# Other column blocks, later selection rounds, a split copy and a reordered first chunk in a retention and soft-MoE kernel

## The chip, the core and the metric

The kernel runs on one core of a Trainium2 chip. The metric is the device time of one execution in microseconds. A profiled execution also gives a span, from the first to the last instruction of the program on the core; the device time is a little longer than the span. All times on a trace below count from the start of the span.

The engines are named as the profile names them: PE is TensorE (matmuls; PEld is its weight load), DVE is VectorE, ACT is ScalarE, POOL is GpSimd, and SP is SyncE, which issues every DMA here. PSUM is the memory that PE writes its results to.

## The reference

Two layers stand behind each other. The first is a retention layer for 4 batches, 8 heads, 768 tokens and head size 64, in which a state per head decays by a factor gamma at each token:

```python
for t in range(S):
    state = gamma * state + k[:, :, t] (outer) v[:, :, t]
    y[:, :, t] = q[:, :, t] @ state / sqrt(D)
```

Its output, with the heads side by side, is x with 3072 tokens of 512 columns. The second layer is a soft mixture of 8 experts with 4 slots each:

```python
logits = x @ phi                               # 3072 x 32
d = softmax(logits, over the tokens)
slot_input = d.T @ x                           # 32 x 512, 4 slots per expert
slot_out = relu(slot_input @ w1[e]) @ w2[e]    # 512 -> 1024 -> 512
c = softmax(logits, over the 32 slots)
out = c @ slot_out                             # 3072 x 512
```

All data is fp32. The weights w1 and w2 have 16.8 MB each, and the output, which the kernel writes transposed as 512 x 3072, has 6.3 MB.

## The kernel before, in words

**Retention.** The work is cut into 24 steps (`NSTEP`): 4 batches of 6 chunks, each of 128 tokens. A step loads three things: `load_kq(i)` brings k and q transposed (512 KB, into one of four tiles `kq`), `load_v(i)` brings v (256 KB, into a tile `h`) and, in some steps, k in its natural order (another 256 KB). On POOL v is then scaled by the decay (L207); for chunk 0 the scaling is split between POOL and DVE instead (L428 to L430). `scores(i)` makes the products of k and q on PE (L225), and DVE multiplies them by a mask (L229) into a tile that `intra(i)` multiplies with v on PE (L258). `inter(i)` adds the part of the carried state (L247), `scale(i)` scales the result on DVE (L267), `state(i)` updates the state (L280, L282), and `natural(i)` transposes the 128 x 512 block of x on PE (L288) and copies it out of PSUM (L290): on ACT for all steps, except for the last step, which uses DVE.

**Routing.** After each group of four steps `logits_mm` and `logits` make the slot logits, with a running maximum, and `dispatch_p` and `dispatch_u` add the group's part of the slot inputs: four matmuls (L342), each of which needs one step's copied x. The last group is finished after the loop, at about 109 to 117 us, and gives the slot inputs `siT` (L520). `combine_weights` makes the combine weights c of a group.

**Experts.** `hidden(g, k)` multiplies the slot inputs with the tiles of w1 (L533): two halves g of four experts each, with four k each. After the last k of a half its two PSUM tiles are copied out, one by ACT (L539) and one by DVE (L540). `hidden_t(g)` transposes the hidden layer (L546) and applies the relu on DVE (L551).

**Selection rounds.** The output matmuls want c with a token along the free axis and a slot pattern along the partitions. `split_c` splits c on DVE into two parts (L384, L385). `c_round(n)`, for n from 0 to 3, multiplies them on PE with selection matrices (L395) into two PSUM tiles named `sm`, of which there are two, and ACT copies them to the tiles `c4T` (L401): four copies in rounds 0 and 1 (which serve the first 2048 tokens), two in rounds 2 and 3. Two rounds in a row thus need the same two `sm` tiles, and a round's matmuls wait until ACT has copied the round before.

**Blocks of columns.** The second expert layer and the output go by blocks of output columns, `BLOCKS`: 128, then 256, then 128. The tiles of w2 are stored and loaded in the order of the blocks. For each block PE runs 64 matmuls (L623: two halves of experts, eight steps `fc` over the 1024 hidden values, four experts each) into one PSUM tile, which needs all of that block's w2. `finish(cb, op)` is a generator that then does the rest: a copy on DVE (L586), a summing matmul (L590), a cast and a subtraction on DVE (L592, L593), and then the output matmuls (L605), two for each output tile of 128 columns by 1024 tokens. Their results are copied by DVE (first half, L611) and ACT (second half, L608), and SP writes the tile of 512 KB to HBM (L609). So a block of 128 columns has 6 output matmuls and 3 writes, and a block of 256 has 12 and 6. Each `yield` of the generator lets the next block run one `fc` step of four matmuls; `Y1` and `Y2` say how many steps lie before the summing matmul and before the first output matmul, and `BURST` says that output matmuls go in threes. When a block's matmuls are through, what is left of the generator before is drained.

**What sets the order.** The order on PE is the order of the code (`ORDERED`). On the other engines a scheduler sets the order when the program is built. Each engine runs its queue in order. SP issues the loads in its queue's order; the ring for weights has 34 tiles of 512 KB (`NRING`), and four more weight loads go to the `kq` tiles and six to pairs of `h` tiles.

Of the kernel before, what the change touches and what calls it, by code (L numbers as in the profile page):

```python
# [12 lines left out]
ALU = mybir.AluOpType  # L13
# [4 lines left out]
C = 128  # L18
# [16 lines left out]
HLOAD = 4  # L35
ORDERED = {mybir.EngineType.PE}
NPRE = 34
BLOCKS = [(0, 128), (128, 256), (384, 128)]
NRING = 34
NHALF = 20  # L40
NSPLIT = 6
# [2 lines left out]
KLOAD = [i for i in range(1, NSTEP) if i % NC in (0, 2, 4)]  # L44
KQW = 1088
FPS = {256: 4, 192: 4, 128: 8, 64: 8}
Y1 = (3, 4, 2)
Y2 = (4, 6, 2)
GRP = 4
NGRP = NSTEP // GRP  # L50

# [40 lines left out]
def retention_soft_moe_kernel(  # L92
# [117 lines left out]
    def scores(i):  # L210
        s = st[i]
        state = i % NC < NC - 1 and i not in KLOAD
        A = s["A"] = [half_tile().rearrange("p (r g t) -> p r g t", r=2, t=C) for _ in range(2)]
        if state:
            s["kn"] = half_tile().rearrange("p (h e) -> p h e", e=D)
        for hf in range(2):
            scv = sct[hf][:, :, 0:384].rearrange("p r (g n) -> p r g n", n=192)
            for gg in range(2):
                g = 2 * hf + gg
                for late in range(2):  # L220
                    for r in range(2):
                        o = (late if g % 2 == 0 else 1 - late) * D
                        kb = KB[2 * g + late]
                        n = 2 + state - late
                        nc.tensor.matmul(scv[o:o + D, r, gg, late * D:(late + n) * D],  # L225
                                         s["kq"][r * D:(r + 1) * D, kb * D:(kb + 1) * D],
                                         blocks(s["kq"], r, NB - (2 - late) * QS[g], QS[g], n),
                                         start=True, stop=True)
            nc.vector.tensor_tensor(A[hf], scv[:, :, :, 0:C],  # L229
                                    mask.unsqueeze(1).broadcast_to([128, 2, 2, C]), ALU.mult)  # L230
            if state:
                kn = s["kn"].rearrange("p (g r) e -> p r g e", r=2)[:, :, 2 * hf:2 * hf + 2]
                nc.scalar.copy(kn, scv[:, :, :, C:C + D])  # L233
# [50 lines left out]
    def natural(i):  # L284
        s = st[i]
        xp = ps.tile([128, DM], F32, name="misc")
        for g in range(NPAIR):
            nc.tensor.transpose(xp[:, g * 128:(g + 1) * 128], s["yT"][:, g, :], ident)  # L288
        s["xn"] = half_tile()
        (nc.vector.tensor_copy if i == NSTEP - 1 else nc.scalar.copy)(s["xn"], xp)  # L290

    gs = {}

# [43 lines left out]
    def dispatch_u(g):  # L337
        q = gs[g]
        last = g == NGRP - 1
        u = ps.tile([128, DM], F32, name="y1" if last else "misc")  # L340
        for j in range(GRP):
            nc.tensor.matmul(u[32 * j:32 * j + 32, :], q["p"][:, 32 * j:32 * j + 32], st[GRP * g + j]["xn"],  # L342
                             start=True, stop=True, tile_position=(0, 32 * j))
        if g == 0:
            nc.scalar.copy(acc, u)
        elif last:
            q["u"] = ysc.rearrange("p g t -> p (g t)")
            for k in range(NK):
                ks = slice(k * 128, (k + 1) * 128)
                nc.scalar.copy(q["u"][:, ks], u[:, ks])  # L350
        else:
            nc.vector.scalar_tensor_tensor(zrun, zrun, q["al"], q["z"], ALU.mult, ALU.add)
            nc.vector.scalar_tensor_tensor(acc, acc, q["al"], u, ALU.mult, ALU.add)


    def combine_weights(g):
# [68 lines left out]
                         nc.const_aps.tensor(0.0, [128, WN], WDT), start=True, stop=True)  # L425
    pe_ = [None]
    scores(0)
    for e, hs_ in ((nc.gpsimd, slice(4, 8)), (nc.vector, slice(0, 4))):  # L428
        e.tensor_tensor(st[0]["v"][:, hs_], st[0]["v"][:, hs_],
                        vsc[:, 0, hs_].unsqueeze(2).broadcast_to([128, 4, D]), ALU.mult)  # L430
    budget = 0.0
    for i in range(NSTEP):
        last = i == NSTEP - 1
# [132 lines left out]
    load_weights(4)  # L566
    hidden(1, 1)
    hidden_t(0)
    c_round(0)
    for k in (2, 3):  # L570
        load_weights(4)
        hidden(1, k)
        c_round(k - 1)
    load_weights(len(weights))
    c_round(3)


    co_tags = [(pe, "sm", 2), (ps, "misc", 1), (ps, "y1", 1), (pe, "sm", 2), (ps, "S", 1)]
# [37 lines left out]

    for cb, (c0, w) in enumerate(BLOCKS):
        op = pe.tile([128, 512], F32, name=("sc0", "sc1")[cb % 2])
        for g in range(2):
            for fc in range(NFC):  # L620
                for j in range(4):
                    t, f = w2t[4 * g + j, cb][2 * fc // FPS[w]], fc % (FPS[w] // 2)
                    nc.tensor.matmul(op[32 * j:32 * j + 32, :w], hT[fc // 2][:, fc % 2, 4 * g + j, :],  # L623
                                     t[:, f * w:(f + 1) * w],
                                     start=(g == 0 and fc == 0), stop=(g == 1 and fc == NFC - 1),
                                     skip_group_check=True, tile_position=(0, 32 * j))
                if cb == 0 and g == 0 and fc == 2:
                    hidden_t(1)
                for f in pend:
                    next(f, None)  # L630
        done = finish(cb, op)
        next(done)
        for f in pend:
            for _ in f:
                pass
        pend = [done]
# [59 lines left out]
```

## Time and profile before

| | us |
|---|---|
| device time, median of 3 runs | 175.55 |
| lowest and highest of them | 175.05, 176.4 |
| device time of the profiled execution | 174.94 |
| its span | 173.0 |
| PE busy | 149.7 (86%) |
| DVE busy | 93.2 (54%) |
| ACT busy | 48.1 (28%) |
| DMA queue of the program, share of 16 engines | 92.9% |

The DMA engines moved 62.51 MB in the span, 361 GB/s on average. PE is busy in most of the span as well. A share over the whole span does not tell which of the two ends last in a stage; for that the span is cut into stages, and in each the waits and the DMA share are read. Three views are used: the busy time by windows, the instructions of one engine in order of time (with the idle time before each, and what ended it), and the chain of work that ended last. A line of the time order gives start and duration in us, engine, line, operation, what is written and read, and how many instructions are merged; a time in square brackets is the idle time before it. On PE an fp32 matmul is recorded as two instructions.

### The profile page before, as it was taken

Reading aid. Unit: us, or ns where it says so; the run is one execution under the profiler, and the core shown is the slowest. Engines: PE = TensorE matmul, PEld = TensorE weight load, DVE = VectorE, ACT = ScalarE, POOL = GpSimd, SP = SyncE. Lnnn points to the kernel's source line nnn. Section 1 sums busy time; section 2 is a strip of 40 time slices with the busy share of each in tenths; the row PEclk is TensorE's granted clock in tenths of the full one; section 3 lists DMA queues with packets and bytes.
Section 4 is the critical chain, followed back from the end, with each engine's and each line's share of the span. In section 5 each row is a group of like instructions: output and inputs, shape, how many; then the busy total and the mean of one; then the engine's idle time right before and its main releaser. Section 6 shows DMA issues by size and latency. Waiting matters only on the chain.

```text
span 173.0 us, 6469 instructions
## 1 busy us (share of the span) xinstructions
PE 149.7 (86%) x2752; PEld 106.4 (62%) x2752; DVE 93.2 (54%) x278; ACT 48.1 (28%) x122; POOL 31.9 (18%) x46
## 2 busy tenths in 40 slices
PE   8589966999899999979999799999977898999700
PEld 2378955689669767868679668853322493566500
DVE  1566645777876787757775685434132131425720
ACT  2133322343513342324133422310102700303510
POOL 0243214213331322031421322400200000000000
PEclk9999999999999999999999999999999999999985
DMA  5999999999999999999999998999999999444993
GB/s 186 322 408 390 368 403 408 403 392 403 402 397 405 403 401 407 396 405 401 403 403 402 406 405 330 279 352 328 357 412 418 410 405 367 184 194 175 393 405 123
DMA packets 20765, 62.51 MB, mean 361 GB/s; under 512 B 2304, under 2 KB 2688, under 8 KB 20736
## 3 DMA queue, kind: packets, MB, share of 16 engines
q1 hardware_dynamic: 20736, 62.09, 92.9%
q8 instruction: 22, 0.36, 0.9%
q14 instruction: 7, 0.06, 0.1%
HBM read 55.79 MB, written 6.29 MB: 359 GB/s over the span
## 4 chain that ended last, share of the span: by engine, by line
PE 69%; DMA 13%; DVE 6%; issue 5%; SPq 1%; ACT 1%; DVEq 0%
PE y L258 11%; PE sc L225 10%; PE sc L623 9%; PE misc L288 7%; PE y L247 5%; DMA kq<-in_kq_dram 5%; DMA r<-in_w_dram 5%; PE y L533 4%; PE S L280 4%; DMA h<-in_v_dram 3%; PE misc L300 3%; PE misc L342 2%; PE misc L533 2%; PE S L533 2%; PE sm L605 2%
## 5 line engine op out<-in xcount | busy, mean ns | idle before, releaser
L229 DVE TENSOR_TENSOR h<-sc,kt 128x512 f32<-128x512 f32 x48 | 31.4, 686 | 18.6 <-PE sc L225 14.6
L207 POOL TENSOR_TENSOR h<-h,kt 128x512 f32<-128x512 f32 x23 | 24.1, 1049 | 61.8 <-DMA h<-in_v_dram 46.3
L267 DVE SCALAR_TENSOR_TENSOR h<-y,kt,ysc 128x128 f32<-128x128 f32 x96 | 27.3, 343 | 4.5 <-PE y L258 4.2
L258 PE MATMUL y<-h 128*64 128x128 f32 x384 | 26.9, 279 | 3.1 <-DVE h L229 2.1
L225 PE MATMUL sc<-kq 64*64 64x128 f32 (+2 forms) x768 | 26.2, 270 | 2.4 <-issue 0.9
L258 PEld LDWEIGHTS y<-h 128*64 128x64 f32 x384 | 20.8, 136 | 11.2 <-issue 6.8
L225 PEld LDWEIGHTS sc<-kq 64*64 64x64 f32 x768 | 21.3, 133 | 7.1 <-issue 4.0
L288 PE MATMUL misc<-kt,h 128*128 128x128 f32 x96 | 15.6, 285 | 2.4 <-DVE cb L361 1.3
L290 ACT COPY h<-misc 128x512 f32<-128x512 f32 x23 | 13.5, 586 | 14.4 <-PE misc L288 12.5
L282 ACT COPY sst<-S 128x256 f32<-128x256 f32 x20 | 7.4, 372 | 33.6 <-PE S L280 33.5
L280 PE MATMUL S<-h 128*64 128x64 f32 x320 | 13.0, 222 | 1.4 <-issue 1.4
L247 PE MATMUL y<-kq,sst 64*64 64x128 f32 x320 | 13.7, 273 | 0.2 <-issue 0.2
L280 PEld LDWEIGHTS S<-h 128*64 128x64 f32 x320 | 12.2, 138 | 1.5 <-issue 1.5
L288 PEld LDWEIGHTS misc<-kt,h 128*128 128x128 f32 x96 | 10.1, 141 | 4.9 <-issue 2.2
L623 PE MATMUL sc<-r,h 128*32 128x128 f32 (+1 forms) x256 | 12.2, 315 | 0.0
L233 ACT COPY h<-sc 128x256 f32<-128x256 f32 x18 | 6.7, 373 | 15.4 <-DVE h L229 15.4
L247 PEld LDWEIGHTS y<-kq,sst 64*64 64x64 f32 x320 | 10.1, 133 | 0.8 <-issue 0.5
L623 PEld LDWEIGHTS sc<-r,h 128*32 128x32 f32 x256 | 7.8, 109 | 4.3 <-issue 2.3
L533 PE MATMUL y<-r,siT 128*32 128x512 f32 x64 | 8.2, 595 | 0.0
L401 ACT CAST r<-sm 128x256 fp32r<-128x256 f32 x12 | 3.7, 383 | 9.9 <-PE sm L395 9.9
L300 PE MATMUL misc<-h,phis 128*32 128x128 f32 x160 | 5.7, 276 | 0.4 <-issue 0.4
L342 PE MATMUL misc<-h,p 128*32 128x512 f32 x40 | 5.3, 605 | 0.0
(122 smaller groups left out, 145.8 us busy)
## 6 DMA issues: line engine op xcount, KB each, us to landing
r<-in_w_dram SPq DMA_DIRECT2D x54, 512.0 KB, 8.4
kq<-in_kq_dram SPq DMA_DIRECT2D x20, 512.0 KB, 7.8
h<-in_v_dram SPq DMA_DIRECT2D x24, 256.0 KB, 7.6
out_dram<-r SPq DMA_DIRECT2D x12, 512.0 KB, 5.4
h<-in_w_dram SPq DMA_DIRECT2D x12, 256.0 KB, 6.6
h<-in_kn_dram SPq DMA_DIRECT2D x11, 256.0 KB, 7.4
kq<-in_kq_dram SPq DMA_DIRECT2D x4, 544.0 KB, 6.4
kq<-in_w_dram SPq DMA_DIRECT2D x4, 512.0 KB, 7.0
```

The lines of the kernel that those rows point to most:

```text
L207: nc.gpsimd.tensor_tensor(v, v, vsc[:, i % NC, :].unsqueeze(2).broadcast_to([128, H, D]), ALU.mult)
L225: nc.tensor.matmul(scv[o:o + D, r, gg, late * D:(late + n) * D], s["kq"][r * D:(r + 1) * D, kb * D:(kb + 1) * D], blocks(s["kq"], r, NB - ...
L229: nc.vector.tensor_tensor(A[hf], scv[:, :, :, 0:C], mask.unsqueeze(1).broadcast_to([128, 2, 2, C]), ALU.mult)
L247: nc.tensor.matmul(y[b][o:o + D, gl, :], sst[r * D:(r + 1) * D, g, :], blocks(s["kq"], r, NB - 2 * QS[g], QS[g], 2), start=(gl == 0), stop ...
L258: nc.tensor.matmul(y[g // 2][o:o + D, g % 2, :], s["v"][:, 2 * g + r, :], s["A"][g // 2][:, r, g % 2, :], start=(c == 0 and g % 2 == 0), s ...
L267: nc.vector.scalar_tensor_tensor(yT[:, g, :], y[g // 2][:, g % 2, :], ybs[:, c, g:g + 1], ysc[:, g, :], ALU.mult, ALU.mult)
L280: nc.tensor.matmul(S_[r * D:(r + 1) * D, g, :], s["kn"][:, 2 * g + r, :], s["v"][:, 2 * g + r, :], start=(c == 0 and g == 0), stop=True, s ...
L288: nc.tensor.transpose(xp[:, g * 128:(g + 1) * 128], s["yT"][:, g, :], ident)
L290: (nc.vector.tensor_copy if i == NSTEP - 1 else nc.scalar.copy)(s["xn"], xp)
L300: nc.tensor.matmul(q["ltp"][32 * j:32 * j + 32, :], phis[:, p, :], st[GRP * g + j]["yT"][:, p, :], start=(p == 0), stop=(p == NPAIR - 1), ...
L533: nc.tensor.matmul(hp[g][half][32 * j:32 * j + 32, :], siT[:, k, :], w1t[4 * g + j, k][half], start=(k == 0), stop=(k == NK - 1), skip_gro ...
L623: nc.tensor.matmul(op[32 * j:32 * j + 32, :w], hT[fc // 2][:, fc % 2, 4 * g + j, :], t[:, f * w:(f + 1) * w], start=(g == 0 and fc == 0), ...
```

## The change

Five things are edited.

1. `BLOCKS` is now 256, 128, 128, and `Y1` and `Y2` go with it. The w2 tiles are stored and loaded in the new order; the number of loads and their sizes stay the same.
2. `c_round(0)` and `c_round(1)` come one step later, behind `hidden(1, 2)` and `hidden(1, 3)`. `c_round(2)` and `c_round(3)` move into the first block's matmuls, behind its steps (0, 6) and (1, 2).
3. The copy of x of the last step is cut in halves of 256 columns, the first on ACT, the second on DVE.
4. The scaling of v of chunk 0 is asked to issue after the second mask multiplication (`issue_after`).
5. The handles `s["am"]` and `q["acc"]` are kept; the second is not used.

```diff
-BLOCKS = [(0, 128), (128, 256), (384, 128)]
+BLOCKS = [(0, 256), (256, 128), (384, 128)]
...
-Y1 = (3, 4, 2)
-Y2 = (4, 6, 2)
+Y1 = (4, 3, 2)
+Y2 = (6, 6, 2)
...
-            nc.vector.tensor_tensor(A[hf], scv[:, :, :, 0:C],
+            s["am"] = nc.vector.tensor_tensor(A[hf], scv[:, :, :, 0:C],
                                     mask.unsqueeze(1).broadcast_to([128, 2, 2, C]), ALU.mult)
...
-        (nc.vector.tensor_copy if i == NSTEP - 1 else nc.scalar.copy)(s["xn"], xp)
+        if i == NSTEP - 1:
+            nc.scalar.copy(s["xn"][:, 0:256], xp[:, 0:256])
+            nc.vector.tensor_copy(s["xn"][:, 256:512], xp[:, 256:512])
+        else:
+            nc.scalar.copy(s["xn"], xp)
...
-    for e, hs_ in ((nc.gpsimd, slice(4, 8)), (nc.vector, slice(0, 4))):
-        e.tensor_tensor(st[0]["v"][:, hs_], st[0]["v"][:, hs_],
-                        vsc[:, 0, hs_].unsqueeze(2).broadcast_to([128, 4, D]), ALU.mult)
+    with tc.issue_after(st[0]["am"].ins):
+        for e, hv in ((nc.gpsimd, slice(4, 8)), (nc.vector, slice(0, 4))):
+            e.tensor_tensor(st[0]["v"][:, hv], st[0]["v"][:, hv],
+                            vsc[:, 0, hv].unsqueeze(2).broadcast_to([128, 4, D]), ALU.mult)
...
     hidden(1, 1)
     hidden_t(0)
-    c_round(0)
     for k in (2, 3):
         load_weights(4)
         hidden(1, k)
-        c_round(k - 1)
+        c_round(k - 2)
     load_weights(len(weights))
-    c_round(3)
...
                 if cb == 0 and g == 0 and fc == 2:
                     hidden_t(1)
+                if cb == 0 and (g, fc) in ((0, 6), (1, 2)):
+                    c_round(2 + g)
```

Three places of the built program show what this moves. Lines of the new kernel are 3 to 5 higher than those of the old for the same statement.

**The rounds, on PE.** Between the first transpose (tile `y`, written from `kt,h`) and the first block's matmuls (`sc<-...,h`), the kernel before has on PE:

```order
L546 MATMUL y_2163<-kt,h 128x128 x4
L395 MATMUL sm<-r 128x512 x4
L533 MATMUL y_2126<-r,siT 32x512 x4
L533 MATMUL S<-r,siT 32x512 x4
L395 MATMUL sm<-r 128x512 x4
L533 MATMUL y_2126<-r,siT 32x512 x4
L533 MATMUL S<-r,siT 32x512 x4
L395 MATMUL sm<-r 128x256 x8
L623 MATMUL sc_2232<-r,h 32x128 x2
```

and the changed kernel:

```order
L551 MATMUL y_2164<-kt,h 128x128 x4
L538 MATMUL y_2127<-r,siT 32x512 x4
L538 MATMUL S<-r,siT 32x512 x4
L399 MATMUL sm<-r 128x512 x4
L538 MATMUL y_2127<-r,siT 32x512 x4
L538 MATMUL S<-r,siT 32x512 x4
L399 MATMUL sm<-r 128x512 x4
L626 MATMUL sc_2217<-r,h 32x256 x2
```

Rounds 0 and 1 (`sm<-r`, 512 wide) each stand behind one more `hidden`, and rounds 2 and 3 (the 256-wide row) are gone from here; they stand as two rows of four inside the first block.

**The same place, on ACT.** `h<-misc` and `h<-y` are the copies of the first and second half of the hidden layer, and the casts from `sm` are those of the rounds. Before:

```order
L498 ACTIVATE wj<-nmc,nms 128x2
L350 COPY ysc<-y_1989 128x128 x4
L362 ACTIVATE cb<-cb 128x128
L539 COPY h<-misc 128x512
L401 CAST r<-sm 128x2x128 x8
L539 COPY h<-y_2126 128x512
L401 CAST r<-sm 128x2x128 x4
L608 COPY r<-misc 128x512
```

Now:

```order
L503 ACTIVATE wj<-nmc,nms 128x2
L291 COPY h<-misc 128x256
L354 COPY ysc<-y_1990 128x128 x4
L366 ACTIVATE cb<-cb 128x128
L544 COPY h<-misc 128x512
L544 COPY h<-y_2127 128x512
L405 CAST r<-sm 128x2x128 x12
L611 COPY r<-misc 128x512
```

The copy of the second half of the hidden layer, which stood behind the eight casts of rounds 0 and 1, now stands ahead of all twelve casts; and the half copy of x stands behind `wj`.

**The copy of x of the last step, on DVE** (`h<-misc`, with what each instruction waits for). Before:

```order
L502 TENSOR_TENSOR zw<-zc,wj 128x2
L290 COPY h<-misc 128x512
L514 TENSOR_SCALAR zi<-sc_2005 128x32 [waits PE_49]
L515 RECIPROCAL zi<-zi 128x32 [waits DVE_49]
L520 TENSOR_TENSOR siT<-sc_2004,zi 128x128 [waits DVE_49,PE_49]
```

Now:

```order
L507 TENSOR_TENSOR zw<-zc,wj 128x2
L292 COPY h<-misc 128x256 [waits Activation_49]
L519 TENSOR_SCALAR zi<-sc_2006 128x32 [waits PE_49]
L520 RECIPROCAL zi<-zi 128x32 [waits DVE_49]
L525 TENSOR_TENSOR siT<-sc_2005,zi 128x128 [waits DVE_49,PE_49]
```

The half copy on DVE waits for ACT, which the whole copy did not.

Two more moves need no rows. At the very end of PE's order, the last block's summing matmul stood behind three output matmuls of the block before; now it stands directly behind 24 of its own block's matmuls, and the last six output matmuls follow it, as they did. On SP some loads of the first third change places: the first, fifth and ninth weight loads now stand ahead of the v loads of chunks 3, 6 and 8, and the k and q load of chunk 11 ahead of the v load of chunk 10; the order of all later loads is the same. On DVE the two mask multiplications of chunk 0 now stand ahead of the scaling of its v.

More of the change, by code (lines that the diff above doesn't have):

```diff
@@ L344, in dispatch_u @@
         if g == 0:
-            nc.scalar.copy(acc, u)
+            q["acc"] = nc.scalar.copy(acc, u)
         elif last:
@@ L352, in dispatch_u @@
             nc.vector.scalar_tensor_tensor(zrun, zrun, q["al"], q["z"], ALU.mult, ALU.add)
-            nc.vector.scalar_tensor_tensor(acc, acc, q["al"], u, ALU.mult, ALU.add)
+            q["acc"] = nc.vector.scalar_tensor_tensor(acc, acc, q["al"], u, ALU.mult, ALU.add)
     def combine_weights(g):
```

## The prediction

> **What bounds the kernel now.** I read the busy time by windows first. A row gives the window, its length, busy time of PE, PEld, DVE, ACT and POOL, the granted PE clock, the DMA share and GB/s.
>
> ```profile
> 0.00:76.00 76.00, 67.16 (x1445) 53.30 (x1449) 49.62 (x135) 24.22 (x59) 19.99 (x28) 1.00 1.00 383
> ...
> 128.00:137.60 9.60, 7.17 (x55) 2.77 (x53) 3.38 (x19) 3.59 (x11) 0.00 (x0) 1.00 1.03 416
> ...
> 148.00:154.00 6.00, 6.00 (x112) 3.44 (x103) 1.48 (x3) 1.07 (x2) 0.00 (x0) 1.00 0.66 265
> 154.00:157.20 3.20, 3.20 (x65) 2.26 (x65) 1.66 (x4) 0.57 (x1) 0.00 (x0) 1.00 0.00 0
> 157.20:163.00 5.80, 4.85 (x68) 3.14 (x61) 3.85 (x8) 2.74 (x6) 0.00 (x0) 1.00 0.84 329
> 163.00:170.00 7.00, 1.59 (x6) 0.85 (x5) 1.89 (x3) 1.63 (x3) 0.00 (x0) 0.81 1.00 399
> ```
>
> Up to 76 us the DMA engines are full, with PE nearly so. From 148 on PE has no gap but the DMA engines starve: idle from 154.0 to 157.2, because only 3 of the 12 output writes can leave after a first block of 128 columns. Then it turns round: after 163 PE is almost done and the DMA engines are full to 170. The end is a backlog of writes. The instructions that issue the writes show the same, first the three of the first block, then the other nine:
>
> ```profile
> L609 SPq DMA_DIRECT2D out_dram<-r x3: 332/344/348, 147.9 to 150.5; - x3
> ...
> DMA to landing us min/median/max: 2.6/2.6/3.6
> ```
>
> ```profile
> L609 SPq DMA_DIRECT2D out_dram<-r x9: 332/332/1088, 157.2 to 165.7; - x9
> ...
> DMA to landing us min/median/max: 2.8/5.5/6.5
> ```
>
> A write on idle DMA engines lands 2.6 us after its issue, the third of a close group 3.6 us. The last one, issued at 165.7, takes 6.5 and lands at 172.2, 0.8 us before the end of the span. So 2.9 us of the end are queueing. The third view is PE in order of time between the hidden layer and the first block:
>
> ```profile
> 128.08 0.60 PE L546 MATMUL y<-kt,h 128*128 128x128 f32 x4
> 130.16 0.50 PE L395 MATMUL sm<-r 32*128 32x512 f32 x2 [1.48 <-DVE r L384]
> 131.15 0.49 PE L395 MATMUL sm<-r 32*128 32x512 f32 x2 [0.49 <-DVE r L385]
> ...
> 133.43 0.73 PE L395 MATMUL sm<-r 32*128 32x512 f32 x4
> 134.09 1.07 PE L533 MATMUL y<-r,siT 128*32 128x512 f32 x8
> ...
> 135.95 0.50 PE L395 MATMUL sm<-r 32*128 32x256 f32 x4
> 136.91 0.77 PE L395 MATMUL sm<-r 32*128 32x256 f32 x4 [0.46 <-ACT r L401]
> 137.60 0.30 PE L623 MATMUL sc<-r,h 128*32 128x128 f32 x2
> ```
>
> Here PE stands idle for 1.48, 0.49 and 0.46 us: round 0 waits for DVE's split of c, round 3 for ACT's copies. None of it is a wait for weights.
>
> **The change part by part**, on the clock of this trace.
>
> *First chunk.* DVE's scaling of v waits for its DMA and holds the masks:
>
> ```profile
> 6.81 0.43 DVE L429 TENSOR_TENSOR h<-h,kt 128x256 f32<-128x256 f32 x1 [1.33 <-DMA h<-in_v_dram]
> 7.15 1.28 DVE L229 TENSOR_TENSOR h<-sc,kt 128x512 f32<-128x512 f32 x2
> ```
>
> ```profile
> 75.59 0.90 PE L225 MATMUL sc<-kq 64*64 64x128 f32 x32 [0.71 <-DMA kq<-in_kq_dram]
> ```
>
> With the masks first, 1.28 us of masks lie in the 1.33 us of waiting, and PE starts on the chunk some 0.5 us earlier. But at 75.59 PE waits 0.71 us for a load whose DMA engines were full all the time before, with the same bytes ahead of it. An earlier PE waits longer there. I take -0.1; bounds -0.6 (all of it passes, as feeding the DMA earlier might let it) and +1.4 (one displaced load comes too late; rivals).
>
> *Copy of the last x.* The fourth matmul of the slot inputs waits for it:
>
> ```profile
> 112.08 0.30 ACT L498 ACTIVATE wj<-nmc,nms 128x2 f32<-128x2 f32 x1
> ```
>
> ```profile
> 112.62 0.68 DVE L290 COPY h<-misc 128x512 f32<-128x512 f32 x1
> ```
>
> ```profile
> L282 ACT COPY sst<-S 128x256 f32<-128x256 f32 x20 | 7.4, 372 | 33.6 <-PE S L280 33.5
> ```
>
> The order shows that DVE's half now waits for ACT's half. ACT's 0.37 starts behind `wj` at about 112.35 and ends at 112.7, DVE's 0.42 (the 256-wide DVE copy at 153.48 below) ends at 113.2, against 113.3 now. I take -0.1; bounds -0.3 (side by side) and 0. [...]
>
> *Rounds.* The split of c ends where it did, so the second half of round 0 still starts at 131.15. `hidden(1, 2)`, 1.86 us by the rows at 134.09 and 135.95, now fits between 128.7 and 130.5, into the two waits of 1.48 and 0.49: it is free, and `hidden(1, 3)` runs from 131.6 to 133.5. Round 1 then waits for both `sm` tiles, and ACT now copies the hidden layer ahead of the casts that free them:
>
> ```profile
> 134.20 1.20 ACT L401 CAST r<-sm 128x256 fp32r<-128x256 f32 x4 [1.34 <-PE sm L395]
> 135.36 0.58 ACT L539 COPY h<-y 128x512 f32<-128x512 f32 x1
> ```
>
> That copy starts 1.27 us after the start of its `hidden` (134.09 to 135.36), so at 132.9, and ends at 133.45; the four casts take 1.20, to 134.65, and the rest of round 1 some 0.5. The first block starts at 135.2 instead of 137.60: **-2.4**. Bounds: -3.4 if round 1 did not wait (133.5 and 0.73), -1.9 if the whole round of 0.73 and more waits follow the casts. What is late next is ACT's work for the rounds, but hidden by 64 matmuls. Rounds 2 and 3 go into the first block, 0.50 each: **+1.0**; their `sm` tiles are free long before.
>
> *Blocks.* The sum of PE's work stays the same: 64 matmuls of 256 columns, 128 of 128, 24 output matmuls. The first block now needs 16 loads of w2 instead of 8, the last four of them the first four of this row:
>
> ```profile
> 119.09 19.74 SPq L171 DMA_DIRECT2D r<-in_w_dram  x20
> ```
>
> ```profile
> r<-in_w_dram SPq DMA_DIRECT2D x54, 512.0 KB, 8.4
> ```
>
> At about 1 us apart and 8.4 us to landing they are there by some 131, before PE asks; the last loads of all, issued by 138.8, land at some 147 and belong to the last block, which stands behind the whole middle block and 12 output matmuls. At the end of PE's order the copy of the last block is no longer covered by three output matmuls:
>
> ```profile
> 153.48 0.42 DVE L586 COPY acc<-sc 128x256 f32<-128x256 f32 x1 [3.16 <-PE sc L623]
> ...
> 160.98 0.28 DVE L586 COPY acc<-sc 128x128 f32<-128x128 f32 x1
> ```
>
> ```profile
> 161.50 0.38 PE L590 MATMUL y<-acc,rep 128*128 128x128 f32 x2
> 162.84 0.47 PE L605 MATMUL sm<-r,h 128*128 128x512 f32 x1 [0.95 <-DVE h L593]
> ```
>
> Its 0.28 and the two handovers now lie bare: **+0.5** (0.3 to 0.7). The way from there to the last six output matmuls, 1.34, stays. They start at 162.84 - 0.1 - 0.1 - 2.4 + 1.0 + 0.5 = 161.7, and the last write is issued at 165.7 - 1.1 = 164.6.
>
> *Writes.* Six writes now leave between the first and second block's end, by the same count about 149 to 154, where the DMA engines had been starving. The three of the middle block follow, the last of them released by the copy behind the second trio of output matmuls; here is what such a trio looks like now:
>
> ```profile
> 156.75 0.86 PE L623 MATMUL sc<-r,h 128*32 128x128 f32 x24
> 157.54 0.50 PE L605 MATMUL S<-r,h 128*128 128x512 f32 x1
> ```
>
> ```profile
> 158.56 0.59 ACT L608 COPY r<-misc 128x512 f32<-128x512 f32 x1
> ```
>
> The copy ends 1.6 us after the trio's start. Between that trio's end and the last six output matmuls lie 24 block matmuls (48 records, twice the 0.8 above), the bare 0.5 and the 1.34: 3.4 us. So the ninth write is issued at about 159.1 and lands at 162.7 at the latest, before the tenth is issued at 163. The last three find no backlog: the last lands 3.6 after its issue instead of 6.5, **-2.9**.
>
> [...]
>
> Sum: -0.1 - 0.1 - 2.4 + 1.0 + 0.5 - 2.9 = **-4.0 us**, a span of 169.0 after 173.0. The profiled execution took 174.94; it becomes 170.9. It lies 0.6 below the median of the runs, so for the median I say 175.55 - 4.0 = **171.5**.
>
> **The rivals.**
>
> *No wait in round 1, and the early start passes.* If ACT's casts came in time, the rounds give 1.0 more, and the first chunk up to 0.5 more: 170.0. Against it: the order on ACT and the wait at 75.59.
>
> *The drain stays.* If the last writes take 6.5 us to land because of PSUM copies and DMA side by side rather than because of the queue, only -1.1 is left: 174.4, within 1%. For it: the median of the nine is already 5.5. Against it: the DMA share of 1.00 from 163 to 170, at 399 GB/s, which is a queue.
>
> *Late loads.* In the first third four loads are displaced behind a load of 512 KB each, which is 1.4 us at the 383 GB/s of the first window. If all four were on the path, that is +5.5, with the rest 177.0: slower. It decides where a v lands less than 1.4 us before its use. The tightest is chunk 3:
>
> ```profile
> 16.71 1.04 POOL L207 TENSOR_TENSOR h<-h,kt 128x512 f32<-128x512 f32 x1 [1.62 <-DMA h<-in_v_dram]
> ```
>
> ```profile
> 20.49 1.09 PE L258 MATMUL y<-h 128*64 128x128 f32 x16
> ```
>
> Scaled at 17.75, used at 20.49: 2.7 us, of which the delay and the earlier PE take 1.9. The others have more. One late load alone would be eaten by the wait at 75.59 in part.
>
> *The block does not help.* If the first block waited for its w2, the writes would move back by the same. The landings above speak against it; it would give some 173.
>
> **How the numbers follow.** Forecast (170.5 to 172.7) 0.60; no wait and early start (near 170) 0.15; the drain stays or the gain is halved otherwise (173.5 to 175) 0.18; late loads 0.04; the rest, unforeseen on either side, 0.03. The likeliest is 171.5. The bounds of the terms, taken together, give about 1.3 either way, and the range reaches a little into the drain's case: 169.8 to 173.7. A measurement of this kernel tells 1% (1.75 us) from no change; faster by more than that means below 173.8: 0.80. Within 1%: 0.15. Slower: 0.05.
>
> **What would show it.** Right: the first block's matmuls start near 135, with ACT's copy of the hidden layer ahead of the casts and an idle time before round 1; no stretch of 3 us with a DMA share of 0 after 150; landings of at most 4 us for the last three writes; the wait for k and q at 75.6 longer than 0.71. Wrong: a last write that still takes 6 us, PE idle before L258 in the first third, or a first block that waits for w2.

## The result, and the profile after

| | before | after |
|---|---|---|
| device time, median of 4 runs each, us | 175.3 (174.96 to 176.4) | 170.56 (170.34 to 170.81) |
| ratio of the times | | 0.972, interval 0.967 to 0.977 |
| profiled execution, us | 174.94 | 170.34 |
| its span, us | 173.0 | 168.6 |

The change makes the kernel 2.8% faster. The forecast was 171.5 for the median and 169.0 for the span. Here and below, single runs over 1.5% above the fastest of their kernel are left out of every ratio and its interval.

PE in order of time between the hidden layer and the first block, after the change:

```profile
128.15 0.60 PE L551 MATMUL y<-kt,h 128*128 128x128 f32 x4
128.68 1.06 PE L538 MATMUL y<-r,siT 128*32 128x512 f32 x8
...
130.53 0.50 PE L399 MATMUL sm<-r 32*128 32x512 f32 x2
131.21 0.50 PE L399 MATMUL sm<-r 32*128 32x512 f32 x2 [0.18 <-DVE r L389]
131.64 1.07 PE L538 MATMUL y<-r,siT 128*32 128x512 f32 x8
...
134.09 1.27 PE L399 MATMUL sm<-r 32*128 32x512 f32 x4 [0.53 <-ACT r L405]
135.29 0.41 PE L626 MATMUL sc<-r,h 128*32 128x256 f32 x2
```

The two waits for DVE's split of c, 1.48 and 0.49 us, have become 0.18; a new one of 0.53 for ACT's casts stands before round 1. The first block starts at 135.29 instead of 137.60. ACT at the same place:

```profile
132.90 0.59 ACT L544 COPY h<-y 128x512 f32<-128x512 f32 x1 [8.74 <-PE y L538]
133.39 1.21 ACT L405 CAST r<-sm 128x256 fp32r<-128x256 f32 x4
```

The copy of the hidden layer runs ahead of the casts, at the 132.9 that the sum had. The end of PE's work:

```profile
159.61 0.49 PE L593 MATMUL y<-acc,rep 128*128 128x128 f32 x2 [0.41 <-DVE acc L589]
160.97 0.47 PE L608 MATMUL sm<-r,h 128*128 128x512 f32 x1 [0.87 <-DVE h L596]
```

The bare copy of the last block costs 0.41, as forecast (0.5). The last six output matmuls start at 160.97 (forecast 161.7, before 162.84). The windows of the last stage, with the same columns as before (length, the five engines, granted PE clock, DMA share, GB/s):

```profile
148.00:154.00 6.00, 6.00 (x96) 3.82 (x99) 3.86 (x8) 3.23 (x6) 0.00 (x0) 1.00 0.76 301
154.00:157.20 3.20, 3.20 (x69) 2.36 (x66) 1.85 (x4) 0.59 (x1) 0.00 (x0) 1.00 1.01 394
157.20:163.00 5.80, 4.30 (x59) 2.70 (x57) 3.02 (x7) 2.33 (x5) 0.00 (x0) 1.00 0.74 290
163.00:170.00 7.00, 0.00 (x0) 0.00 (x0) 0.43 (x1) 0.41 (x1) 0.00 (x0) 0.66 0.57 226
```

From 154.0 to 157.2 the DMA engines are now full; before they stood still there. In the last window they work for 0.57 of the time instead of all of it. The writes by groups of three, from SP's issues (middle group 156.5, last group 162.4):

```profile
L612 SPq DMA_DIRECT2D out_dram<-r x3: 332/332/354, 156.5 to 158.4; - x3
DMA to landing us min/median/max: 4.1/4.9/5.6
```

```profile
L612 SPq DMA_DIRECT2D out_dram<-r x3: 332/332/511, 162.4 to 163.5; - x3
DMA to landing us min/median/max: 3.0/3.6/4.2
```

The last write is issued at 163.5 and takes 4.2 us, after 6.5 before.

### The profile page after: what moved, and what is told of

It is laid out like the page before. It is cut to its first block, busy times and chain, and to the rows that moved or that the text cites. A ratio compares the mean times of both kernels' runs of the same rounds, so it can differ in the third digit from the quotient of the medians.

```text
span 168.6 us, 6471 instructions
## 1 busy us (share of the span) xinstructions
PE 150.7 (89%) x2752; PEld 106.2 (63%) x2752; DVE 93.5 (55%) x278; ACT 48.5 (29%) x123; POOL 31.6 (19%) x46
## 4 chain that ended last, share of the span: by engine, by line
PE 80%; DVE 9%; issue 5%; ACT 2%; DVEq 0%; POOL 0%; ACTq 0%; POOLq 0%
PE sc L225 13%; PE y L258 13%; PE sc L626 9%; PE misc L288 8%; PE y L247 6%; PE S L280 5%; PE y L538 4%; PE misc L304 3%; PE misc L428 3%; PE misc L346 2%; PE misc L538 2%; DVE h L229 2%; PE sm L608 2%; DVE h L267 2%; PE sm L399 1%
## 5 line engine op out<-in xcount | busy, mean ns | idle before, releaser
L225 PE MATMUL sc<-kq 64*64 64x128 f32 (+2 forms) x768 | 26.7, 270 | 2.4 <-issue 1.5
L288 PEld LDWEIGHTS misc<-kt,h 128*128 128x128 f32 x96 | 10.1, 141 | 5.3 <-issue 2.1
L626 PE MATMUL sc<-r,h 128*32 128x128 f32 (+1 forms) x304 | 12.7, 292 | 0.0
L626 PEld LDWEIGHTS sc<-r,h 128*32 128x32 f32 x304 | 8.3, 109 | 4.4 <-issue 2.7
L304 PEld LDWEIGHTS misc<-h,phis 128*32 128x32 f32 x160 | 4.2, 109 | 2.5 <-issue 2.5
```

The source lines that it names most:

```text
L304: nc.tensor.matmul(q["ltp"][32 * j:32 * j + 32, :], phis[:, p, :], st[GRP * g + j]["yT"][:, p, :], start=(p == 0), stop=(p == NPAIR - 1), ...
```

## Experiments

All times are device times; "before" beside them is the kernel before on the same chip, whose median over all runs there was 176.6 (first four kernels) and 176.5 (next four), with most single runs between 174 and 178 and one of 769. The last four were run once each, the three behind the stop at 144 us on other chips, where the kernel before took 174.8 and 177.1 in a run each.

**Blocks alone, rounds alone.** The kernel before with one part of the change each.

```diff
-BLOCKS = [(0, 128), (128, 256), (384, 128)]
+BLOCKS = [(0, 256), (256, 128), (384, 128)]
-Y1 = (3, 4, 2)
-Y2 = (4, 6, 2)
+Y1 = (4, 3, 2)
+Y2 = (6, 6, 2)
```

> The kernel before with the new blocks alone (256, 128, 128, and Y1, Y2). If the terms add up as forecast, the first block starts at 137.6 as before, the last six output matmuls come 0.5 us later or, without the 0.8 us stall of TensorE that the kernel before had at 143, some 0.3 earlier, and the last write lands 3.6 to 4.2 us after its issue instead of 6.5: 2 to 3 us faster than before, about 172.9. Rival, the writes are all that counts and the rounds add nothing: the whole gain of the change, 170.6. Rival, the blocks only help when the rounds have made room: no gain, 175.3.

```diff
-    c_round(0)
...
-        c_round(k - 1)
+        c_round(k - 2)
-    c_round(3)
...
+                if cb == 0 and (g, fc) in ((0, 6), (1, 2)):
+                    c_round(2 + g)
```

> The kernel before with the later rounds alone, blocks of 128, 256, 128 as before. If the terms add up: the first block starts 2.3 us earlier, rounds 2 and 3 cost 1.0 us in it, so everything behind, the backlog of nine writes included, moves by 1.3 to 1.4 us: about 173.9, with a last landing of still 6 us or more. Rival, the end is set by the writes alone: they move with the first block's output matmuls, so the same; but if the weights' transfers hold them, under 0.5 us of gain.

Blocks alone took 173.52 in the median of all six runs (ratio 0.979, 0.967 to 0.991), rounds alone 172.87 (0.984, 0.977 to 0.991). But the runs of the first spread from 170.8 to 175.1: three took 170.78, 171.60 and 173.19, the other three 173.85 to 175.14. Its profile, of a run near the upper end, holds a piece that has nothing to do with blocks:

```profile
132.13 0.49 PE L395 MATMUL sm<-r 32*128 32x512 f32 x2 [1.47 <-DVE r L384]
133.12 0.77 PE L395 MATMUL sm<-r 32*128 32x512 f32 x2 [0.50 <-DVE r L385]
133.82 1.94 PE L533 MATMUL y<-r,siT 128*32 128x512 f32 x8
```

```profile
133.20:136.60 3.40, 3.40 (x18) 0.78 (x18) 0.00 (x0) 1.20 (x4) 0.00 (x0) 0.50 1.02 410
```

Behind the two waits of round 0 the granted clock was 0.50 for 3.4 us: eight matmuls took 1.94 us instead of 1.06. The profile of rounds alone has the same 3.4 us at 0.50 behind the first chunk's wait, at 10.5 us. So a wait of PE may cost more than its length, in some executions and not in others: in the first profile of the kernel before, with waits of 1.48 and 0.49 us at the same place, the granted clock stays at 1.00 from 128.0 to 137.6. The drain came as expected: the last write landed 4.1 us after its issue with the blocks alone, and 6.2 with the rounds alone.

**The same with the waits filled.** To take that out, idle matmuls were put into the first chunk's wait and into the one before round 0, in the kernel before and in each part alone (with the rounds alone only the first, since `hidden(1, 2)` stands in the second wait there).

```diff
+    for _ in range(FILL0):
+        nc.tensor.matmul(wp[0:WM, 0:WN], nc.const_aps.tensor(0.0, [128, WM], WDT),
+                         nc.const_aps.tensor(0.0, [128, WN], WDT), start=True, stop=True)
...
+    for _ in range(2):
+        ft = pe_[0].tile([128, 4, 128], F32, name="sc1")
+        for j in range(4):
+            nc.tensor.transpose(ft[:, j, :], ident, ident)
```

> The kernel before with idle work for TensorE in two gaps: three small matmuls of zeros behind the first scores, and eight transposes of the identity ahead of round 0. They compute nothing that is used. In the profile of the blocks alone TensorE's clock was granted at a half for 3.4 us from 133 on, behind the 2 us of waiting for round 0; in that of the rounds alone from 10.5 on, behind the first chunk's wait. If these drops are what makes runs of the kernel before differ by 4 us, the fill gives a granted clock of 0.985 or more in nearly every run, a spread under 1 us and a median of 174 to 174.5 on a chip where the kernel before has 176.6. Rival, the difference comes from elsewhere: median and spread as those of the kernel before.

> The same fill, and the new blocks alone. With the clock held, this shows the blocks' own part. By the terms: 2.9 us less of drain, 0.5 more on TensorE, so 2.4 us under the kernel with the fill alone; 3.0 to 3.2 if the stall of 0.8 us at 143 also goes. Rival, the writes are all that counts: all of the change's gain, that is, within 0.4 us of the changed kernel.

> The first fill, and the later rounds alone. By the terms 1.4 us under the kernel with the fill alone, 2.2 if the stall at 143 also goes, with a last landing of still 6 us or more. Rival, under 0.5 us, since the backlog of writes stays.

| filled | us | lowest to highest | ratio to before, interval |
|---|---|---|---|
| before | 175.31 | 174.19 to 177.67 | 0.999, 0.994 to 1.003 |
| blocks | 172.46 | 172.11 to 173.91 | 0.984, 0.977 to 0.991 |
| rounds | 172.86 | 172.20 to 173.12 | 0.984, 0.978 to 0.989 |

The filled kernel before was to fall to 174.0 to 174.5 with a spread under 1 us. It did neither: its runs spread over 3 us, and its ratio holds 1. What the fill did do is hold the clock: 11 of its 12 runs had a mean granted clock of 0.983 or more, against 7 of the 16 others of the kernel before. In the kernel before, those 7 took 174.23 to 175.95 and all others 176.16 and more, so there the clock and the time go together. But the 11 filled runs still lie between 174.19 and 176.49, and what spreads them is not settled.

Without its longest run, of 177.67, the filled kernel before has a median of 175.13. Against this, blocks are worth 2.7 us and rounds 2.3, together 4.9, about what the change gives (4.7). In the profiles, PE stands idle for 0.87 us at 145.0 in the filled kernel before, and in neither of the two others, so such a sum counts this gain twice (the section on the stop at 144 us tells what it is). From the first block to the last six output matmuls, without that idle time, the three profiles take 24.01 (139.28 to 164.16, less 0.87), 24.55 with blocks and 24.97 with rounds: +0.54 and +0.96, the +0.5 and +1.0 of the prediction. From the first matmul of the hidden layer to the last landing the profiles show 53.9 us for the filled kernel before, 51.6 with blocks and 52.0 with rounds; without fill it is 55.0 before and 50.5 with the whole change. The last three writes, blocks first, then rounds:

```profile
L617 SPq DMA_DIRECT2D out_dram<-r x3: 332/333/527, 163.9 to 165.0; - x3
DMA to landing us min/median/max: 2.7/3.5/4.1
```

```profile
L611 SPq DMA_DIRECT2D out_dram<-r x3: 332/1037/1137, 162.4 to 164.1; - x3
DMA to landing us min/median/max: 5.2/5.9/6.0
```

The short landing comes with the new blocks, and the rounds alone do not bring it.

**The first chunk.** The changed kernel without `issue_after`:

```diff
-    with tc.issue_after(st[0]["am"].ins):
-        for e, hv in ((nc.gpsimd, slice(4, 8)), (nc.vector, slice(0, 4))):
+    for e, hv in ((nc.gpsimd, slice(4, 8)), (nc.vector, slice(0, 4))):
```

> The changed kernel with the scaling of the first chunk's v ahead of the masks again, as before. In the two traces the changed kernel is 0.7 us ahead at 75 us and no longer ahead at 111 us. If that lead is always lost to TensorE's own stalls, undoing the edit costs nothing: 170.6, within 0.3. If the lead normally reaches the end and the loss was chance, it costs 0.5 to 0.7: 171.2. Rival, the displaced loads cost something: it gains.

170.84 us (ratio 0.973, 0.967 to 0.979), a span of 168.6 like that of the changed kernel. The edit gives nothing that can be measured.

**ACT's copy ahead of the casts.** The changed kernel with both copies of the second half of the hidden layer on DVE, so that nothing stands before the casts on ACT.

```diff
-            nc.scalar.copy(hs[g][0], hp[g][0])
+            (nc.vector.tensor_copy if g else nc.scalar.copy)(hs[g][0], hp[g][0])
```

> The changed kernel with both copies of the hidden layer's second half on VectorE, so that the casts of round 0 on ScalarE no longer stand behind one of them. If round 1 waits for those casts as forecast (0.53 us of idle time and a round of 1.27 instead of 0.73), the first block starts near 134.3 instead of 135.3, and the time falls by 0.9: 169.7. Rival, the writes and the last loads share the DMA engines until 148.7, so that the end does not follow: 0.3 or less. Rival, round 1 waits for something else: the idle time before it stays.

```profile
132.61 1.04 PE L538 MATMUL S<-r,siT 128*32 128x512 f32 x8
133.58 0.73 PE L399 MATMUL sm<-r 32*128 32x512 f32 x4
134.25 0.41 PE L626 MATMUL sc<-r,h 128*32 128x256 f32 x2
```

Round 1 waits for nothing more, takes 0.73 instead of 1.27 with its inner wait, and the first block starts at 134.25, 1.04 earlier. The kernel takes 169.66 us (ratio 0.966, 0.961 to 0.972), the lowest of all here that compute everything; its interval overlaps that of the change, and the spans are 167.3 and 168.6. On the same chip the changed kernel without `issue_after` took 170.39 to 171.29, and every run of this one lies below (169.24 to 170.05).

**The first six writes left out.** The changed kernel, where the first block's results are not written.

```diff
+                        if cb > 0:
-                        nc.sync.dma_start(out[...], ot[0:mw])
+                            nc.sync.dma_start(out[...], ot[0:mw])
```

> The changed kernel without the six writes of the first block; it leaves that half of the output unwritten. If the drain is a queue on the DMA engines, the seventh write lands 2.6 to 2.8 us after its issue instead of 4.1, the ninth after 3.6 instead of 5.6, the last after 3.6 instead of 4.2, and the time falls by about 0.6. Rival, a write beside copies out of PSUM takes its 4 to 6 us anyway: landings and time as in the changed kernel.

The middle and the last group of three in this kernel:

```profile
L613 SPq DMA_DIRECT2D out_dram<-r x3: 343/347/355, 157.0 to 159.0; - x3
DMA to landing us min/median/max: 2.7/4.7/5.4
```

```profile
L613 SPq DMA_DIRECT2D out_dram<-r x3: 332/332/502, 162.9 to 164.0; - x3
DMA to landing us min/median/max: 2.7/3.5/4.1
```

The seventh write lands in 2.7 instead of 4.1 us, so in the changed kernel it still queues behind the first six. The last lands in 4.1, hardly less than 4.2: what is left there is no backlog of the first six. The group's own spacing gives it: three writes issued within 1.13 us, landing 2.7, 3.5 and 4.1 us after their issue, some 1.25 us apart. The eighth and ninth take 4.7 and 5.4 with nothing ahead of them but their own group. In the changed kernel's trace a packet of the instruction queue is on its way from 158.85 to 160.75, while its middle group lands; whether such a packet holds the writes up was not tested. The time did not fall by the 0.6 that was expected: the one run took 171.54, and from the first hidden matmul to the last landing its profile has 50.4 us, the changed kernel's 50.5. Since the last write takes 4.1 us without a backlog too, there was little to gain.

**The stop at 144 us.** The last six matmuls start 0.73 earlier than forecast. In the kernel before there was one idle time in the stretch between, which the sum had carried along:

```profile
144.13 0.62 PE L623 MATMUL sc<-h 128*32 128x256 f32 x2 [0.81 <-issue]
```

Nothing that the profile shows released it, and the changed kernel's profile has none behind 117 us. All idle times of over 0.3 us put down to issue, in all profiles here, stand at few places when TensorE's records are counted from the first (those of its sequencer included, some 105 of 5609, which the windows leave out): 706, 962, 1474, 1730, 2242, 2498, 3010, 3778 and 5058, or one record before: 706 + 256 k. The windows show it without that count. Kernel before up to the stops at 77.5 and 144.1; the filled kernel before up to stops at 79.0 and 145.0:

```profile
0.00:77.45 77.45, 68.31 (x1474) 54.09 (x1474) 50.83 (x137) 24.22 (x59) 19.99 (x28) 1.00 1.00 383
...
0.00:144.10 144.10, 130.16 (x2480) 94.74 (x2480) 82.80 (x258) 41.49 (x110) 31.90 (x46) 1.00 1.00 382
```

```profile
0.00:79.00 79.00, 71.16 (x1474) 54.59 (x1474) 51.03 (x137) 24.26 (x59) 21.07 (x29) 1.00 1.00 381
0.00:144.98 144.98, 133.72 (x2480) 95.84 (x2480) 82.97 (x258) 41.54 (x110) 31.77 (x46) 1.00 0.99 377
```

1474 and 2480 matmul records both times, although the filled kernel has idle matmuls in front, so that other matmuls of the program have these numbers. The second of its stops reads

```profile
145.01 1.07 PE L631 MATMUL sc<-h 128*32 128x256 f32 x16 [0.87 <-DMA r<-in_w_dram]
```

and names a load, but the w2 tiles that this matmul reads had landed some 20 us before: a landing that fell into the idle time by chance. The DMA queues have a kind of their own for instructions:

```profile
q1 hardware_dynamic: 20736, 62.09, 92.9%
q8 instruction: 22, 0.36, 0.9%
```

22 packets of 16 KB: one for each 256 records (5609 / 22 = 255; the 0.36 MB over 5609 records are 64 bytes a record). The idle times at these numbers end 1.2 to 1.6 us behind the end of a packet. That holds for some that the profile puts down to another engine as well: at 962 every profile with all its loads has 1.3 to 1.9 us, mostly put down to DVE. At 144 us the packet ended at 142.65, PE went on at 144.13; the stretch of 256 before had taken 4.8 us of work, matmuls of 128 columns while the DMA engines were still full of loads (a share of 1.03 from 138.56 to 143.32). Three kernels went after this.

The kernel before once more, unchanged:

> The kernel before, profiled once more. Theory of the instruction packets: its first block of 128 columns uses up 256 instructions in about 4.9 us while the DMA engines are still full of weight loads, so a stop near record 5058, early in the second block, should be there again, between 0 and 1.2 us by how soon the packet came, and no stop of PE without a releaser at any other place behind 117 us. Rival (the 0.81 us at 144 us was an accident of one execution): no stop there, or one at another number.

It took 176.66 us. The stop is there at the same number, with 0.22 us, and nowhere else behind 117:

```profile
139.70 0.30 PE L623 MATMUL sc<-r,h 128*32 128x128 f32 x2
...
145.64 0.62 PE L623 MATMUL sc<-h 128*32 128x256 f32 x2 [0.22 <-issue]
...
164.35 0.47 PE L605 MATMUL sm<-r,h 128*128 128x512 f32 x1 [0.95 <-DVE h L593]
```

From the first block to the last six it needs 24.65 us, and the first profile of before 25.24: the difference of 0.59 is that of the stops. This run also had the half clock behind the waits of round 0 (eight matmuls in 1.94 us at 132.42), which is why it is longer all the same.

The changed kernel with fewer early loads of weights:

```diff
-NPRE = 34
+NPRE = 12
```

> The changed kernel with 12 instead of 34 weight loads spread over the retention steps; the other 22 follow later, so the experts will wait for weights and the whole time will be far longer, some 185 to 200 us; it is not what is read here. Read are the idle times of PE that the profile puts down to issue. In the profiles of before, of the change and of the six others they stand at records number 706 + 256 k of PE and PEld (706, 962, 1474, 1730, 3010, 3778, 5058), whichever matmul of the program has that number, and each ends 1.3 to 1.6 us behind the end of an instruction packet of 16 KB on the DMA engines (16 KB are 256 instructions of 64 bytes). Theory (PE waits for its next 256 instructions, whose packet stands in line behind full DMA engines): with DMA engines that are not full between 20 and 100 us the packets come within 1.5 us of the record number that starts a stretch instead of 2.5 to 4.4, and the idle times behind issue, 5.2 us in sum between 15 and 110 us in the changed kernel, fall below 1.5. Rival (PE stops at every so many instructions whatever the DMA engines do): they stay at 4 to 6 us at the same numbers. Second rival (the stops belong to the program, a wait that the profile doesn't show): they stay at the same matmuls.

It settles nothing: SP issued loads of weights early all the same, the DMA engines kept a share of 0.99 between 20 and 100 us, and the time was 176.56, not 185 or more. Two stops behind issue were left, 1.75 and 2.03 us, at 706 and 1730: numbers of the row (the changed kernel has five, 4.2 us in sum, not the 5.2 of the expectation), but with the DMA engines as full as before they tell nothing of the cause.

So the loads were taken away, all but the first tile of weights:

```diff
-            if which == "w1":
-                src = w1[e, k * 128:(k + 1) * 128, :]
+            if nld[0] == 0:
+                if which == "w1":
+                    src = w1[e, k * 128:(k + 1) * 128, :]
...
+                t1.extend(t)
+            t = t1
```

> The changed kernel with only the first of the 64 loads of w1 and w2: every tile of weights is that one, so 63 loads of 512 KB are left out, and with them the products are of other numbers; PE runs the same matmuls in the same order. The DMA engines then carry some 22 MB in the retention part, about 210 GB/s instead of 400, and nothing but the writes behind it. It asks what the kernel with fewer early weight loads did not answer, since its DMA engines stayed full (0.94 to 1.03 of their time between 20 and 100 us). Theory (PE's next 256 instructions stand in line behind full DMA engines): PE has no stop behind issue over 0.3 us at records 706 + 256 k; the packets come within 1.5 us of the start of a stretch. The first hidden matmul starts at some 112 instead of 117.2 us, and the end is some 5 us earlier or more. Rival (PE stops at every so many instructions whatever the DMA engines do): 4 to 6 us of stops remain at the same numbers, the first hidden matmul starts at 116 to 117 us.

PE's waits of this kernel between 20 and 100 us, all of them (line waited for: us in total, times, longest), and then those of the changed kernel behind issue in the same window, with the one at record 962 above them:

```profile
PE misc L291 <- DVE lb L335: 1.1, 4, 0.5
PE misc L291 <- DVE acc L360: 0.5, 1, 0.5
PE misc L291 <- PE S L283: 0.4, 1, 0.4
```

```profile
PE misc L288 <- DVE cb L365: 1.6, 1, 1.6
PE sc L225 <- issue: 1.5, 2, 0.9
PE misc L304 <- issue: 1.4, 1, 1.4
PE S L280 <- issue: 0.7, 1, 0.7
PE y L258 <- issue: 0.6, 1, 0.6
```

No idle time put down to issue is left, at any number. One that is put down to a matmul, 0.45 us at 26.39, stands at 962 and ends 1.38 us behind the end of a packet, which was on its way from 24.0 to 25.0, with a DMA share of 1.07: most likely a last stop, where the DMA engines were full for a moment. Together the stops fall from 5.8 us (962 included) to 0.45. In the same 80 us PE gets through more, with half the DMA traffic; this kernel first, the changed one second:

```profile
20.00:100.00 80.00, 77.99 (x1759) 63.83 (x1757) 60.55 (x177) 27.63 (x74) 24.09 (x29) 1.00 0.63 207
```

```profile
20.00:100.00 80.00, 72.75 (x1603) 58.77 (x1603) 55.65 (x160) 26.38 (x70) 21.42 (x23) 1.00 1.03 402
```

The first hidden matmul starts at 108.95 instead of 117.22, 3 us earlier than expected. PE's idle time up to there falls from 10.1 to 5.0 us, about what the stops lose; the other 3.2 us are shorter busy time of PE (103.95 instead of 107.15) for the same matmuls, and their cause is open. The rival that PE stops at every so many instructions, 4 to 6 us in sum whatever the DMA engines do, falls. Not all packets came within 1.5 us, as had been expected: some came 2 to 3 us behind the start of a stretch, and nearly all of them in time. The last three writes, which no load disturbs here, land in 2.7, 3.5 and 4.1 us again.

## Why the prediction was right, and where it was not

| on the trace, us | before | forecast | after |
|---|---|---|---|
| first hidden matmul | 117.15 | 116.95 | 117.22 |
| first block | 137.60 | 135.0 | 135.29 |
| last six output matmuls | 162.84 | 161.7 | 160.97 |
| last write issued | 165.66 | 164.6 | 163.49 |
| its landing | 172.17 | 168.2 | 167.72 |

**Rounds: right, by their own steps.** -2.4 were forecast from the first hidden matmul to the first block and -2.38 came: two waits gone, one new one, with ACT's copy as its cause. Taking that copy off ACT brought the first block forward by 1.04 us, the 1.0 that the upper bound had set for it.

**Blocks: the mechanism right, the drain mis-sized by 0.6.** The idle DMA stretch is gone and the last landing takes 4.2 instead of 6.5. I had taken 3.6, the third of the first group in the kernel before, but that group is issued over 2.6 us and the last one over 1.1. By its own spacing the third lands 2.7 + 2 x 1.25 - 1.1 = 4.1 us after its issue, and six other kernels with these blocks show 4.1 (the one with fewer early loads 7.6). Single writes on idle DMA engines still land in 2.65 to 2.7 (2.69 and 2.65 for the first two in the changed kernel, 2.7 for the first of each group with the first six left out). The middle group was not free of backlog either: its last write lands at 164.1, not at 162.7, and so after the tenth is issued.

**From the first block to the last six: a term that was missing.** Forecast were 25.24 + 1.5 = 26.7 us; it took 25.68. Of the 1.06 too much, 0.81 are the stop at 144 us. I saw it in the trace and took the stretch with it as PE's work. In the changed kernel the stretch of 256 at that place takes 7.0 us, and PE does not stop; but the slower stretch is not what saved it in this profile. There the packet ended 2.3 us behind the start of the stretch, and with some 1.4 us more (stops end 1.2 to 1.6 us behind a packet) PE could, by this estimate, have gone on in time even after 4.8 us. In the two profiles of the kernel before the packets ended 4.1 and 3.7 us behind, too late for 4.8. Both kernels with rounds alone keep the narrow matmuls, use up the stretch in 4.6 and 4.9 us and do not stop, with packets that ended 3.0 and 3.4 us behind. Only in the filled kernel with the blocks (3.7 behind, a stretch of 7.4) did the slower stretch decide. Why the packet came sooner is open. Shown is that the two profiles of before differ in this stretch by what their stops differ (0.59), and that the stops all but vanish when the DMA traffic goes (0.45 us at a share of 0.63, after 5.8 at 1.03). The other 0.25 are not settled.

**First chunk: the wrong reason, and luck in the number.** I had PE start earlier and give it back at a wait for k and q at 75.6 that would grow. That wait is gone: PE reached the place at 74.81 instead of 75.59, and the loads came some 0.7 us earlier too. The lead was then lost in the next rows:

```profile
74.81 0.90 PE L225 MATMUL sc<-kq 64*64 64x128 f32 x32
77.81 0.96 PE L304 MATMUL misc<-h,phis 128*32 128x128 f32 x26 [1.45 <-issue]
```

A stop for instructions of 1.45 us instead of 0.35, at 3010. Such a stop ends behind its packet (here 1.28 us behind it, 1.42 in the kernel before), so an earlier PE waits longer: PE came 0.80 us earlier (76.36 instead of 77.16), and the packet itself ended 0.45 later (76.54 instead of 76.09). An earlier PE that only waits longer is what I had said of the loads, and another queue did it. The four matmuls that wait for the last copy of x began 0.27 later than before (112.52 after 112.25) and took 1.95 us instead of 2.16, so the first chunk came out at +0.3 where I took -0.1, and the copy gave 0.2 where I took 0.1. That the first hidden matmul came so near the forecast is luck: in the profiles with all loads it starts between 117.2 and 119.4, with these stops at different lengths. The halves ran one behind the other, as the order said:

```profile
112.55 0.36 ACT L291 COPY h<-misc 128x256 f32<-128x256 f32 x1
```

```profile
112.95 0.42 DVE L292 COPY h<-misc 128x256 f32<-128x256 f32 x1
```

**The rivals.** The drain does not stay (4.2), no block waits for w2, and no load of v comes late enough for PE to wait for it. That round 1 would not wait fell too, in the changed kernel.

**The sum.** The errors +0.29 (first block), -1.06 (stretch), -0.30 (the last write comes 2.52 us behind the last six instead of 2.82) and +0.63 (drain) make -0.44: a span of 168.6 for 169.0. That errors of up to 1.06 cancel to this is luck in part. The median came out 0.94 lower than forecast, more than the span: I had added 0.6, by which the median of three runs before lay above the profiled execution; after the change it lies 0.2 above, and a fourth run of before put its own median at 175.3. Some runs of before pay for the half clock behind round 0 (eight matmuls in 1.94 us instead of 1.06 in its second profile), and the later rounds leave no such wait; that this makes up the rest is not shown, since the filled kernel before still spread by 2.3 us with its clock held.

## What to carry to other kernels

An idle time without a releaser is not PE's work: count records up to it, and if such places lie 256 apart, as here, look at when the packet of instructions came, how fast the stretch before used its instructions and how full the DMA engines were. Size the drain of a last group of writes by its own spacing (4.1 us here), not by the landing of another group (3.6). Where a wait is removed, look up what the engine that released it has queued ahead: here one copy on ACT held back the first block by another 1.0 us.

## What the runs showed of the hardware

- The instruction queue brought 22 packets of 16 KB for TensorE's 5609 records, over the same DMA engines as the data: the page of before gives it 0.9% of the time of the 16 engines, and 92.9% to the data. With these full (a share of 1.03 between 20 and 100 us in the changed kernel), PE stood for 0.3 to 2.0 us at several of the 22 boundaries of each run, 5.8 us in sum in the changed kernel; at a DMA share of 0.63 on average, at one, for 0.45 us.
- The granted clock fell to 0.50 for 3.4 us behind waits of PE of 1.47 and 0.50 us with a half microsecond of matmuls between, in two profiles out of three with these waits, behind one of 3.1 us (rounds alone), and 1.3 us after the end of one of 2.03 (fewer early loads). One of 2.01 us, with the blocks alone, had no such fall behind it.
